# A new planner's order, with its engine and buffer choices, for a fused attention and squared-ReLU kernel

## The chip, the cores and the metric

The kernel runs on one core of a Trainium2 chip. The metric is the device time of one execution in microseconds (us), lower is better. Before the change, three runs took 608.24, 609.28 and 611.04 us, median 609.28. The engines are named as in the profile: PE is TensorE's matmuls, PEld its weight loads, DVE is VectorE, ACT is ScalarE, POOL is GpSimd, and SP is the engine whose queue issues every transfer (DMA) of this kernel.

## What is computed

Attention with rotary embedding on q, k, v of shape (4 batches, 8 heads, 576 rows, 64), and then a two-layer network on its 2304 x 512 output. In short:

```python
q_rot, k_rot = (rotate(q), rotate(k))
scores = scale * np.matmul(q_rot, k_rot.transpose(0, 1, 3, 2))
attn = softmax(scores)                 # with the row maximum taken off
x = heads_side_by_side(np.matmul(attn, v))     # (2304, 512)
h = x @ w_in                           # (512, 2048)
g = s * np.maximum(h, 0.0) ** 2 + b
return g @ w_out                       # (2048, 512)
```

## The kernel before

The 32 heads are worked on as 16 pairs (pair = two heads of one batch). A pair's 576 rows are 8 tiles of 128 rows (four of each head) and a ninth, number 8, that holds the last 64 rows of both heads. The output rows are nine units: units 0 to 7 are halves of a batch's first 512 rows, and unit 8 is the last 64 rows of all four batches. The network's hidden layer has 16 blocks of 128 columns.

The work is cut into **pieces**, of one to some tens of instructions each. The ones that the text names are these.

- Loads: `load_x` (L530) brings q, k or v of a pair, `load_w` (L447) one of 32 weight chunks of 512 KB, `load_tab` (L533, L534) the rotation table and an identity.
- Weights: `w_low`, `w_rebias` and `w_join` rebuild float32 words from the 8-byte numbers of a chunk, `w_gram` (L477) is a product that bounds their size, and later `w_hi` and `w_lo` split each chunk into two float16 parts.
- Pairs: `rotate` is three steps (L589, L591, L593). Pairs 0 to 3 then go in float32: `qk_T` transposes q or k on TensorE (L766, L769) and `qk_ev` copies the result out. The other pairs are split into float16 by `qk_hi` and `qk_lo`, transposed by a DMA, and k's swapped copy is made by another (`swap_k`). `v_hi` and `v_lo` split v.
- Scores: `s_pair` (L654) or `s_tile` (L672, L673) makes them, `s_max` (L679, L681) the row maximum, `s_exp` the exponentials and row sums, `p_s` and `p_r` (L708) the reciprocal. `p_a` and `p_b` split a tile of probabilities into two float16 parts, and `p_t` and `p_tt` (L738, L742) are transposes by DMA of the result. Some tiles of pairs 0 to 3 are transposed on TensorE instead: `p_diag` makes a diagonal matrix, `p_T` (L794, L796) multiplies with it and `p_ev` copies out. `pv_sum` (L759) and `pv32` (L813) are the products with v, `o_out` writes them into the unit's x.
- Network: `x_norm`, `x_add` (two steps, L845), `x_sum` (L851), `x_scale`, `x_hi` and `x_lo` scale and split a unit's x. `mlp_in` (L886) is one hidden block, `mlp_r` applies ReLU and square, `g_hi` and `g_lo` (L904) split the result, `mlp_out` (L962) adds a block to an output row part, `out_sum` scales it and `store` (L982) writes it out. Unit 0 does this in float32 (`mlp_in0` L912, `mlp_out0` L929). Unit 7 is the last; its output has a full-width part 0 (128 x 512) and two half-width parts 1 and 2 (128 x 256), other units have two full-width ones.

Casts, activations and scaled copies go through helpers, so many pieces share the lines L411, L413 and L416 (`ts_`, `stt`) and L419 (`act`); they are told apart by their tiles.

What sets the order: a function `plan` lists all 2,644 pieces with what they depend on and the engines on which they may run. A search that ran ahead of time wrote three strings into the file. `ORDER` has two characters for each piece, and the program issues the pieces in just that order; each engine then runs its own in that order, waiting at each for what it needs. `PICKS` names an engine (S for ScalarE, V for VectorE, G for GpSimd) for each piece with a choice, and `SLOTS` a buffer for each tile whose kind has several. The main lines (L1005 to L1016) are:

```python
        for n in order:
            x = work[n]
...
                if k[0] in BUFS and k not in at:
                    at[k] = int(next(where))
...
            if x["pick"]:
                a = (*a, pick[x["fn"], a])
```

The choices that matter here are in `plan`:

```python
        add((DVE, POOL), "x_add", u, steps=2, w=[("g", ("n", u))])
            add((DVE, POOL), "g_lo", u, f, r=[("hr", c)], w=[("g", c)])
                add((ACT, DVE, POOL), "p_a", *c, r=[("p", c), ("r", (pr, g))], p=[("pab", c)])
```

Of the kernel before, what the change touches and what calls it, by code (L numbers as in the profile page):

```python
# [42 lines left out]
    "JwJjD-KND1JpB_JxJEJ4BtJqCSJrBsJsJkD3BJEIKAEaBOJtBuCOEMKBJ5JlB2JuEWJyBPKOKCCNBUJzEkBZJ6J0CPJ7CUBaCBKPKaJmJ1ElKQCTJ8BqKbJ9"
    "BvJ2EyCVEJKcKDKiK8J3KXD7KECCacKdCDKeBwCHKFB4afKfKjK9aeB3CEK-adbuD4BxEBKrB5agKkKgCXahCIKYKsaoK_KlKzKZKhKmCJLAJ-ECamK0KnBz"
    "LiKtEDKoEECKapByEFEGLjENEYCAKuCFLkB0anLBKvEOEPLIKwK1aqCGEwK2arKpLVCYCZKxbvaiKqKGK3LJajLWbwLCJ_awLlK4LKazEmCiEZCdCaLFEzbx"
    "byEbLmbzEhLnb0KHLGayEiKyLHLoakLLKIEQK5alLMLTLNaxCtCeLUFLEjCbERCWa0LuLOa1b1LQK6CjLXL7asK7LPCcLYLvLcLZEcbIEdLRL8bFLDEeCvLd"
# [1046 lines left out]
```

## Time and profile before

| | us |
|---|---|
| median of three runs | 609.28 |
| the profiled execution's own time | 608.72 |
| its span, first to last instruction | 606.9 |
| PE busy | 579.2 (95%) |
| DVE busy | 468.6 (77%) |
| ACT busy | 396.2 (65%) |
| POOL busy | 152.0 (25%) |

The profile is of one execution. A row of a group of instructions gives its line, engine, operation, tiles written and read, shapes and count, then its busy time, and what its engine waited for just before. A matmul's end is modelled and overlaps the next one's start, so a stretch in which PE is busy throughout can still hold short waits.

### The profile page before, as it was taken

The numbers are of one execution on the slowest core, as the hardware profiler recorded it, in microseconds if no ns is written. First come the engines' busy times: TensorE is split into PE (matmuls) and PEld (weight loads), VectorE is DVE, ScalarE is ACT, GpSimd is POOL, SyncE is SP. The second block draws the span as 40 slices with busy tenths as digits, with TensorE's granted clock in tenths as the row PEclk, the third lists the DMA queues.
The fourth block names the chain that finished last, engine by engine and source line by source line (L and its number), as shares of the span: only waits on it lengthen the run. The fifth ranks groups of instructions, "written<-read, shape, count | busy, mean of one in ns | idle before, by whom it ended". The sixth has DMA issues, their size and how long they took to land.

```text
span 606.9 us, 12363 instructions
## 1 busy us (share of the span) xinstructions
PE 579.2 (95%) x4655; PEld 394.4 (65%) x4655; DVE 468.6 (77%) x972; ACT 396.2 (65%) x832; POOL 152.0 (25%) x147
## 2 busy tenths in 40 slices
PE   2778999999999999999999999999999999999997
PEld 1556776675776658665866676567666686666774
DVE  5988999998999999888998879988858743413212
ACT  3687897878789887888766767666653555432430
POOL 0155432432213333232413322122010101210100
PEclk9989999999999999999999999999999999999999
DMA  8887899996976477898969498687641223540010
GB/s 339 288 293 252 230 227 196 230 188 145 167 136 170 103 151 176 162 229 184 184 113 172 115 194 153 122 169 155 138 111 22 59 65 50 114 79 1 1 36 35
DMA packets 210011, 90.32 MB, mean 149 GB/s; under 512 B 192288, under 2 KB 196768, under 8 KB 209952
## 3 DMA queue, kind: packets, MB, share of 16 engines
q1 hardware_dynamic: 209952, 89.54, 64.4%
q8 instruction: 36, 0.59, 0.4%
q14 instruction: 23, 0.19, 0.1%
HBM read 31.97 MB, written 4.72 MB: 60 GB/s over the span
## 4 chain that ended last, share of the span: by engine, by line
PE 76%; DVE 11%; DMA 4%; ACT 3%; issue 2%; POOL 2%; SPq 0%; DVEq 0%; ACTq 0%; POOLq 0%
PE px L886 24%; PE po L962 21%; PE px L759 8%; PE s L672 6%; PE po L929 4%; PE px L912 3%; PE s L654 3%; DMA pt<-pab 3%; DVE wio L416 2%; DVE pab L416 2%; PE s L962 2%; DVE s L681 1%; POOL g L845 1%; PE po L794 1%; PE px L477 1%
## 5 line engine op out<-in xcount | busy, mean ns | idle before, releaser
L886 PE MATMUL px<-xa,wio 128*128 128x256 f16 x1536 | 181.4, 273 | 0.0
L962 PE MATMUL po<-wio,g 128*128 128x512 f16 x720 | 172.0, 380 | 0.0
L886 PEld LDWEIGHTS <-wio 128*128 128x128 f16 x1536 | 147.3, 98 | 31.0 <-issue 2.4
L419 ACT ACTIVATE p<-s,nm 128x576 f32<-128x576 f32 x144 | 105.5, 734 | 60.1 <-DVE s L681 34.4
L416 DVE SCALAR_TENSOR_TENSOR pab<-p,sum,pab 128x576 f16<-128x576 f32 x136 | 113.3, 844 | 17.6 <-ACT pab L419 10.0
L962 PEld LDWEIGHTS <-g 128*128 128x128 f16 x816 | 75.9, 98 | 73.3 <-issue 3.8
L681 DVE TENSOR_SCALAR_CACHE_REDUCE s<-s,sc 128x576 f32<-128x576 f32 x108 | 87.8, 819 | 13.7 <-PE s L673 12.0
L413 POOL TENSOR_SCALAR pab<-p,sum 128x576 f16<-128x576 f32 x53 | 50.0, 948 | 157.2 <-DVE sum L708 84.1
L419 ACT ACTIVATE hr<-px,xc 128x512 f32<-128x512 f32 x64 | 43.7, 683 | 67.2 <-PE px L886 58.3
L904 POOL TENSOR_TENSOR g<-hr,g 128x512 f16<-128x512 f32 x29 | 36.8, 1272 | 165.8 <-ACT g L419 90.4
L419 ACT ACTIVATE pab<-p,sum 128x576 f16<-128x576 f32 x64 | 48.1, 765 | 7.9 <-DVE sum L708 6.2
L759 PE MATMUL px<-pt,v 128*64 128x320 f16 (+2 forms) x640 | 50.9, 281 | 1.8 <-DMA pt<-pab 1.6
L419 ACT ACTIVATE hr<-hr 128x512 f32<-128x512 f32 x68 | 42.7, 628 | 1.7
L759 PEld LDWEIGHTS <-v 128*64 128x64 f16 x640 | 34.5, 110 | 13.2 <-issue 10.2
L904 DVE TENSOR_TENSOR g<-hr,g 128x512 f16<-128x512 f32 x35 | 26.0, 742 | 21.9 <-ACT g L419 21.5
L672 PE MATMUL s<-qkT 128*128 128x512 f16 (+1 forms) x120 | 41.5, 383 | 0.0
L672 PE MATMUL s<-kS,qkT 128*128 128x512 f16 (+1 forms) x120 | 41.4, 381 | 0.0
L672 PEld LDWEIGHTS <-qkT 128*128 128x128 f16 (+1 forms) x240 | 22.4, 100 | 24.8 <-issue 4.9
L783 DVE CAST g<-hr 128x512 f16<-128x512 f32 x27 | 11.3, 423 | 35.0 <-ACT hr L419 20.5
L912 PE MATMUL px<-x,wio 128*128 128x128 f32 x256 | 33.0, 281 | 0.0
L912 PEld LDWEIGHTS px<-x,wio 128*128 128x128 f32 x256 | 30.4, 192 | 3.4 <-issue 2.1
L416 DVE SCALAR_TENSOR_TENSOR wio<-x,wio 128x512 uint32<-128x512 uint32 x32 | 26.2, 823 | 5.7 <-POOL wio L413 5.4
(153 smaller groups left out, 831.3 us busy)
## 6 DMA issues: line engine op xcount, KB each, us to landing
x<-in_moe_w_in_dram SPq DMA_DIRECT2D x16, 512.0 KB, 5.1
x<-in_moe_w_out_dram SPq DMA_DIRECT2D x16, 512.0 KB, 4.6
st_v<-in_v_dram SPq DMA_DIRECT2D x16, 320.0 KB, 3.8
st_q<-in_q_dram SPq DMA_DIRECT2D x16, 288.0 KB, 3.8
st_k<-in_k_dram SPq DMA_DIRECT2D x16, 288.0 KB, 4.1
out_dram<-o SPq DMA_DIRECT2D x7, 512.0 KB, 4.0
kS<-qkT SPq DMA_DIRECT2D x24, 144.0 KB, 2.8
pt<-pab SPq DMA_TRANSPOSE x152, 2.9
```

The lines of the kernel that those rows point to most:

```text
L413: eng.tensor_scalar(out=out, in0=in0, scalar1=s1, scalar2=s2, op0=op0, op1=op1)
L416: nc.vector.scalar_tensor_tensor(out=out, in0=in0, scalar=scalar, in1=in1, op0=op0, op1=op1)
L419: nc.scalar.activation(out=out, in_=in_, func=func, **kw)
L654: nc.tensor.matmul(ps[h][:, to], d["qF"][hh, t * P:(t + 1) * P], d["kF"][hh, keys], start=True, stop=True)
L672: nc.tensor.matmul(ps[rows, MAIN:2 * MAIN], lhs, kk[:, h:8:2], start=(n == 0), stop=(n == 1))
L681: nc.vector.tensor_scalar(out=T["s"], in0=T["s"], scalar1=st[pr]["es"], scalar2=None, op0=ALU.mult, op1=ALU.min, accum_out=T["nm"])
L759: nc.tensor.matmul(o[64 * h:64 * h + 64, c], v_rows(pr, h, k, z), p_rows(pr, 2 * (i // 4) + h)[:, k, c], start=((z, k) == todo[0]), stop=( ...
L886: nc.tensor.matmul(ph, w16[0][:, f, wz, cc], X["xa"][:, xz, c], start=(c == 0 and n == 0), stop=(c == NC - 1 and n == 2))
L904: (nc.vector if eng == DVE else nc.gpsimd).tensor_tensor(out=g[:, 1], in0=r, in1=g[:, 0], op=ALU.subtract)
L912: nc.tensor.matmul(ph, wi[:, f + 1, c * P:(c + 1) * P], xs[0]["x"][:, c, j * P:(j + 1) * P], start=(c == 0), stop=(c == NC - 1))
L929: nc.tensor.matmul(X["po"][:, j * DM:(j + 1) * DM], gs["h", j, f - f % 4][:, f % 4 * P:(f % 4 + 1) * P], wo[:, f + 1], start=(n == 1), sto ...
L962: nc.tensor.matmul(po, g[:, gz, jj], w16[1][:, f, wz, to], start=(n == 1 and i == 0), stop=(n == NF and i == 2))
```

## The change

Only the three strings change. `plan`, all pieces and all buffers' counts and sizes stay. Cut to the first lines of each string:

```diff
--- before.py
+++ after.py
 ORDER = (
-    "AvA0AAC0CzADDPDQAOA2A1AxA3AwAZAyAzApC6C7C8C3AEC_C4C5DADCDTAFC9AGDWA4AeC-DDDUAPDBI0DXAQDVAaAqI1ARI2I8BbAbDZDYI3ArAcI9DIDd"
-    "AgDEAIDbI-DJC1DfDKDRDFBdDGDaI4A5AfDNI5DHDcAsAJDLAhBgDODmATAKDeAHBcI6DMDnBeJFI_DoAkJAI7ALDSJGBFDgBiBhC2D8JNJHDhAUJIJOJJBj"
...
+    "C0AACzApDCAvDPADA0C6C7C3C8ArC4C_AqAsC5DQAxAODIC9AwDTDAAyC-DUBbAFI0DBDJAEDfDVA1I1AGI2DWAZI3DZI8AQAPA2DXDaDdARBdDYBgI4A3Db"
+    "I5BcDFAII9DKDeDGDNAbBeAaDHAHBFDcC1DmDODLDDAcBhDRDnBiAeDgDMBjAJJFAkDpI-AKDoI6JNBHBGALJOC2JGATI7DsD8DqJHI_DrDEJIJAAMDtBIDS"
...
 )
...
 PICKS = (
-    "SSSGSSVGSGSGSSSVVGSVSSGGGSSGVVSSVVSSVVSSVVSSVVVSSGGGGGGSGVVGGSVGGSSVVSSGVVSGGVVSGGVVSGGVVSSGVVSGVVVSSSVVVSSVVSGSSGSVSSSS"
...
+    "SSGVSGSSSGGVGGSVSSVVSGGGSGGSGGSSVVSSVVSSVVSSVVSVGGSGVGSGSVVSSSVGSSSGVSSSVVSGSVVVSVVVGSSVVSSVVVGGSVGSSSVVVGSVGGVSSSSSSSSS"
...
 )
...
 SLOTS = (
-    "010021131000100001120001030101111123110010202100013101023000100210133000111110021011201100203130011001202111030013103030"
...
+    "000111230100001101010001201100013101011020232110010230003131102000011010120331010001110002100131200102130101110132012001"
...
 )
...
```

Decoded with the unchanged `plan`, both orders hold the same 2,644 pieces, and in both no piece stands before one that it depends on. Of the 530 choices of an engine 239 go to ScalarE (233 before), 168 to VectorE (166) and 123 to GpSimd (131); of 1,040 buffer choices 591 differ. On TensorE the order of 645 of 705 pieces differs, on average by 5 places and at most by 46. What the text comes back to:

| | before | after |
|---|---|---|
| first transfers | weight chunks 8 and 9, table and identity, q of pair 0, k of pair 0, weight chunk 0 | q of pair 0, table and identity, k of pair 0, weight chunk 7, q of pair 1, weight chunk 8 |
| first on TensorE | `w_gram` 8, `qk_T` q and k of pair 0 | `qk_T` q and k of pair 0, `s_pair` of pair 0 |
| first on VectorE | two `w_join`, then the rotation of q and k of pair 0 | the rotation: two steps of q, one of k, the last of q, one of k, a `w_join`, the last of k |
| `x_add` on GpSimd | units 1, 2, 4, 5, 7, 8 | unit 1 |
| `rotate` on GpSimd | q and k of pair 4, q of pair 6 | q of pairs 4, 6, 13 and 15, k of pair 7 |
| `p_diag` on GpSimd | 5 of 8 | 3 of 8 |
| `p_a` on ScalarE, VectorE, GpSimd | 64, 19, 53 | 67, 25, 44 |
| `w_hi` on the same | 21, 3, 8 | 14, 7, 11 |
| last product and store of unit 7 | part 2 (128 x 256) | part 0 (128 x 512) |

## Rows read from the trace of the kernel before

**Rows 1.** The page's parts 1 and 2: busy us, and TensorE's busy tenths in 40 slices.

```profile
PE 579.2 (95%) x4655; PEld 394.4 (65%) x4655; DVE 468.6 (77%) x972; ACT 396.2 (65%) x832; POOL 152.0 (25%) x147
PE   2778999999999999999999999999999999999997
```

**Rows 2.** Busy time by stretch: stretch, length, busy us of each engine (instructions), granted clock, DMA.

```profile
0.00:60.00 60.00, 40.07 (x306) 28.73 (x307) 48.81 (x90) 39.77 (x85) 18.05 (x21) 0.97 0.84 293
60.00:165.00 105.00, 103.08 (x853) 71.93 (x851) 99.28 (x207) 82.42 (x185) 37.16 (x37) 1.00 0.92 200
165.00:290.00 125.00, 124.05 (x1008) 81.28 (x1006) 117.80 (x252) 104.82 (x221) 37.43 (x33) 1.00 0.73 164
290.00:450.00 160.00, 159.10 (x1328) 106.72 (x1327) 140.12 (x297) 107.67 (x235) 40.07 (x39) 1.00 0.74 147
450.00:607.00 157.00, 152.94 (x1171) 105.78 (x1169) 62.55 (x130) 61.54 (x109) 19.24 (x18) 1.00 0.24 49
```

**Rows 3.** The chain that ended last, in order of time: start us, us, what.

```profile
67.54 1.39 PE px L813 x20
...
163.39 5.24 PE px L886 x48
...
288.32 2.62 PE px L886 x24
...
482.14 2.59 PE po L962 x12
```

**Rows 4.** Timeline of VectorE where units 1 and 3 begin: start us, us, instruction.

```profile
161.49 1.28 DVE L416 SCALAR_TENSOR_TENSOR xa<-x,xs,xa 128x1024 f16<-128x1024 f32 x1
...
164.49 1.54 DVE L416 SCALAR_TENSOR_TENSOR pab<-p,sum,pab 128x576 f16<-128x576 f32 x2
...
286.38 1.28 DVE L416 SCALAR_TENSOR_TENSOR xa<-x,xs,xa 128x1024 f16<-128x1024 f32 x1
```

**Rows 5.** Timeline of the start, SP's queue, VectorE and TensorE.

```profile
0.74 0.87 SPq L447 DMA_DIRECT2D x<-in_moe_w_in_dram  x2
...
2.60 0.74 SPq L530 DMA_DIRECT2D st_q<-in_q_dram  x1
...
6.59 0.69 DVE L416 SCALAR_TENSOR_TENSOR wio<-x,wio 128x512 uint32<-128x512 uint32 x1 [5.41 <-POOL wio L413]
...
8.22 0.75 DVE L589 TENSOR_TENSOR z<-st_q,tab 128x576 f32<-128x576 f32 x1
...
10.61 1.12 PE L766 MATMUL s<-ident,st_q 128*128 128x128 f32 x4 [1.64 <-DVE st_q L593]
```

**Rows 6.** Busy time of the stretch from 5 to 10 us (columns as in rows 2).

```profile
5.00:10.00 5.00, 0.61 (x4) 0.34 (x4) 3.01 (x5) 1.99 (x4) 0.64 (x1) 1.00 1.03 400
```

**Rows 7.** The instructions of line 845: duration ns min/median/max, first and last start, forms.

```profile
L845 POOL TENSOR_TENSOR g<-g x12: 668/1152/1571, 155.8 to 545.4; 128x512 bf16<-128x512 bf16 x6, 128x256 bf16<-128x256 bf16 x6
L845 DVE TENSOR_TENSOR g<-g x4: 291/359/426, 280.6 to 460.0; 128x512 bf16<-128x512 bf16 x2, 128x256 bf16<-128x256 bf16 x2
```

**Rows 8.** TensorE's waits after 60 us: us in total, times, longest us.

```profile
PE px L759 <- DMA pt<-pab: 1.6, 4, 0.7
PE px L851 <- POOL g L845: 1.5, 3, 0.8
```

**Rows 9.** Timeline of the end: the full-width and the last half-width out_sum.

```profile
600.85 0.75 DVE L416 SCALAR_TENSOR_TENSOR o<-po,xc,bcs 128x512 f32<-128x512 f32 x1 [4.70 <-PE po L962]
...
603.53 0.48 DVE L416 SCALAR_TENSOR_TENSOR hr<-s,xc,bcs 128x256 f32<-128x256 f32 x1 [1.22 <-PE s L962]
```

**Rows 10.** DMA issues: tiles, queue, operation, count, KB each, median us to landing.

```profile
out_dram<-hr SPq DMA_DIRECT2D x2, 128.0 KB, 1.9
out_dram<-o SPq DMA_DIRECT2D x1, 256.0 KB, 2.6
```

**Rows 11.** Timeline of VectorE: a rotation step that runs beside one of GpSimd's.

```profile
36.74 1.97 DVE L593 TENSOR_TENSOR st_q<-st_q,z 128x576 f32<-128x576 f32 x1
```

More of the change, by code (lines that the diff above doesn't have):

```diff
@@ L43 @@
[L43 to L46, printed above, removed]
@@ new lines @@
+    "D1KMJVJ4JqBoJrEID-JsJxJkBZJyBpBUEaCNBJBaJtCSKACOKNKBCPKOJlJ5JuB2D6EJJzBtBOBsJ0KCJ6BuEkCBKaJ1EWKDKPKXJmKEJ7J2KbCUB3BPKiKc"
+    "CTBvBqKFKjK8KQKdJ3D7KkCCCDafbuJ8EBKeK9adCEK-acElBxB4KfJ9aeK_CVEZKrKlKgCHKmagBwB5ahKYELKsapKhKzByaoKnKtEManBzKoKZB0KuamK0"
+    "CtD4CFK1CiaqLiLAJ-arCAK2LjECaiK3CGLkKvK4KpLBEDEhLIJ_KqEECJEFLlEGLCCIEPajKGLJENbvakCjLVKwalLmLKCKLnLWCXawbwKxFMEbazbxLoCu"
+    "LFbyEOCvCkbzCwEwb0KHLGaxLTKyEmLUasb1K5LHayEiLuEQa0CoCYEjFLatLLERLXEzLML7LQaua1LYLvLNLcavLRKIE7K6LwLdLZMILDE8K7EcClbFMJLS"
@@ new lines @@
+    "bGb2EdLaMKbIEeLeEfLOL8bHEgb3MLFOLPLrb4CZMMb5bJLEa9MNLsbKb6L5a8LbEpb7a7EnCaa6L6Eyb8MOCdCqbLL9EqLta2E9a-ExMRESFYa_CpFZLfL-"
+    "LxMCL_LyMSL2MACeLzCWMfMBCbMTa3CrL3a4LpL0Mga5CcLqCfMDMULhLgCgE0L4EoB6CQE-B1MhCLbAL1CRMib9bBE_MjB7MEMkCxMVMoCsbQMlMWFKbPMm"
+    "ErMXFaM3b-CyMYMcMZMFFAM4ETNFM5MdE1MuMnb_MHMGMpbRNGcAMQMvEtE2bME3MwE4MaMPbNFNE5MxE6MycBbSMzMbcCChM0bTM6MqbUcDFDCmM7cEbaFP"
+    "MeFEbZM8CncFM9EsbbM-NHNCM_NlEucGFVbONmNIbccHACFBEUNiNJbdNKNDMrNLbeNjNncINANOFQbCM1NPNkbDcJMsM2NoNMNUcKNXNpFRNVNqNNbVFWNY"
@@ new lines @@
+    "NWbWNBcLMtFHN1FXbkN2NtNQcMbjNuNZblcNNENaN3EVNybmcOABNbFCNfbXFSFFFTNrNcOAFUbncPNRbocUNzcQFlNgN0cRcVbYN4NvNScWN5NddBODcXbf"
+    "FGcYFbcZdCOBbgOENhOCdDbhFccSN6dEbiNeFddFdGOFbpdHdIdJNsdKOGbqdLFedMbrcTFIOHdNbscaOLF_OTFfcbbtOQOIN7dOccN9OUbEdPFmcdNTFkFo"
+    "N-NwOVceORdQdRcfPMN_NxOMd2dScgFhdTONPNdZGCchOSN8OJdYciOWPOOXEvFgOedad3PPcjdbF-GMOKdcOhckFndUFyd4djGNFid5cld6diOicmOYOfd7"
+    "ObdtGOOjdddkcndVdldXdfPQOcPROuFzOOOgFjcoPSdhOPOdcpOkdWcqeBGadmcrGAdnOvOxcsdsOlOyOmOpctdeOwFvdgOZdudoOqdvO_OaOzeAFwcuOnOr"
@@ new lines @@
+    "O8GBcvdpO0FxOocwdrFJdweUeCdxPAFpeVO1O9PBO5cxO-dqO6eDPYcyeWOsPCPDczPEPHPZO2dzGJPaPVPIeEd1OtPFeFPjeXFqd9PWPGeLPkPXc0PJF0Pl"
+    "eKO3Frc1O4Pmd_Fsc2FtPbFuPcPndyF3PdO7QAGKPod0PeG0Pgd8eYPhd-GDF4P0PpeMPKPqP1GZPrPuc3eZeNeHQBeOPTP2eGePGEeIc4PfGFGGPsQCeJPv"
+    "QLF1PieRc5PLQOehQMPwc6QPQNeiPtQQejP9F2QRP3eQc7P4PUQSGHP-QTQWekQoGdGIeTP5elF5emc8enP6ebeoP_epQXeSc9eqeaerQDesQEQpQzQFPxQq"
+    "etQIF6Q0QcF7QUeuF8QdQ1GLevPzGRGYc-PyQVQJede5c_QeQGdAewRQQKGPexecQfGQQlfMeyQYQmezRRe4QnP7QgeeQhfNefe6QHQre7QsQiREGbGSP8fD"
@@ new lines @@
+    "Gce8RSRFe9GTfCQtGjfOe0QwfPQxe1GyGzQuQ2RGGee3GffEGgGme_fFRHRNRIQ3QZfQQ4GnRJGhGiGoQ5fXG1QvGkGrQ6ROQ7e2QkRKe-Q8ReRPQyfWfGQ-"
+    "GlfHRTQaQ9RfRbG3fARUQ_QbRVfYfIRcRAfZfhGpRgGVRdQjfBGqRYfJRWHMfgG9RhGsfKRifRGtRjR9G-fiR6fLfjR7RBRmGUR-R8RkRvRnRDRMGvfTRZfa"
+    "fVRoG_G2fbfrRwRCRLHAfqRxR_HBRaRsfkSAF9G4fdflRXSYSBRtSFfSSCSZfURlRuG5SDfcSbSGSaHOffGwScfsfnRyftRzSKG6HNG7HPG8feHCSdRpfuSL"
+    "fvHFHGR3f1RqSEHDR4gBf0GWR0RrR1fmGuf2gCSNgDHEf3gEfpHnf4gFSHfogGSMSef5SfSOfwSgfygHgISPgJR2f6gKHJSQfxgLSjgMfzSkR5f7SRgNSVSr"
@@ new lines @@
+    "HmHQf9HHSWgOSsHaStgZHbShSoS5SpgPHXSqgYSugQGXHIgRS6S2SSSIHceggagSgbSTgTHRgjS3SiSJHYS7HSgiSXS4HZHTS8SvHUTXSwHVSUS9gcf8S-f_"
+    "HpTUHWS_SzHdSlg3gkTYgdglTVg2HKTZSxHfTBTGg4hKTHg5GxTWhLHgTag6f-Smg7S0TkSnSyTbTfgUhMTlTIgWTATChNgVTgTmTJS1gXTcTnHegfgmTKgs"
+    "TDToTLTpT-gnHoTMgtHqIBTNTdICTRH0T_geUATtH1TEguTugvTSTOUMTTghUNggHxThgogwHygqUOHLgpHrTPTwgrTqTvTQhBTxTFTegxTyhAUPUQIEURgA"
+    "TzUST7IAgzT8Hhg1T0T9T1T4UYg9IFUZH2U0UBhCUCTiU1hDUDUGT5gyT2U2T6g0UEUag8IcTjHsUmHtUHhhUjg_UIUkU3hEhVUnUlhFUFHzUog-UVUphOT3"
@@ L84 @@
+    "nonrnunx"
 )
 PICKS = (
[L87 to L90 removed]
@@ L92 @@
+    "VVSVSGSGVGVGVGVSVGSVSVSVSVSGVVSGVVVGSVVGVGSVSVVVSV"
 )
 SLOTS = (
[L95 to L98 removed]
@@ L104 @@
+    "00025120100011100110011001100200101002000110312100101010102000110100121000110100"
 )
```

79 lines of the change are left out of this document (28 added, 51 removed).

## The prediction, made before the changed kernel ran

> **What bounds the kernel now.** I read the busy shares first, then the stretches, then the chain, then the waits. TensorE is busy 95% of the 606.9 us span, and its slices are full from the fifth on [rows 1]. By stretches it idles 19.9 us of the first 60, 1.9 of the next 105, 1.0 and 0.9 in the two after these, and 4.1 in the last, which holds the final stores [rows 2]. So nearly all that an order can win without taking work away is in the first 60 us, at the end, and in short waits. VectorE has little to spare either: it idles 5.7 us of 60 to 165, 7.2 of 165 to 290, and only then falls off [rows 2]. Until about 290 us two engines are nearly full, and a piece moved on VectorE shifts what TensorE can start.
>
> TensorE's products run at their full pace once fed: 48 first-layer products take 5.24 us, or 109 ns each, and 12 second-layer ones 2.59 us, or 216 ns [rows 3]. No product is removed or added, so that time is fixed. The profiled execution took 608.72 us with a span of 606.9, and the median of the three runs, 609.28, lies 0.56 above it. I sum against 608.72 and add 0.56 at the end. About 0.5%, or 3 us, is what a measurement of this kernel can tell from no change.
>
> **How the orders are compared.** Both orders decode to the same 2,644 pieces: 705 on TensorE and 286 on the DMA queue in each; VectorE goes from 859 to 862, ScalarE from 651 to 657, GpSimd from 143 to 134. Sums of work hardly move, so only the order counts. For a chosen product I count what stands ahead of it: on TensorE all pieces before it, on VectorE all pieces up to the last one that it needs. A piece costs the distance from its start to the next start where nothing waits. Two p_b together last 1.54 us [rows 4], so one costs about 0.73.
>
> **The start.** Before, the queue sends two weight chunks (1,024 KB), the table, the identity and then q of pair 0; VectorE's first work is two w_join, from 6.59, the first rotation step of q starts at 8.22 and TensorE transposes q at 10.61 [rows 5]. After, q and the table go first and the first weight chunk fourth. The stretch from 5 to 10 us moves 400 GB/s [rows 6], so 1,024 KB less ahead is worth up to 2.6 us: the first rotation step can start near 5.6, which is VectorE's first work and 1.0 sooner than 6.59. The transpose of q came 2.39 us after that step's start and now has one more step ahead (k's first, 0.75 us): 8.75, or 1.9 sooner. Between 1.0 and 1.9 I take 1.5 for VectorE; the ends are 0 and 2.6.
>
> **The order up to unit 3,** at three places.
> (a) The last float32 value product, pv32(3,0), which starts at 67.54 [rows 3]. VectorE has 84 pieces ahead instead of 90: two s_max, two p_ev, two w_join, one p_s and one p_r fewer, two rotation steps more. That is 3.0 us less; TensorE has two w_gram (0.4 us) less. With the early start TensorE would have lost 4.1 us less by here.
> (b) The first product of unit 1, at 163.39 [rows 3], behind x_lo, which starts at 161.49 and takes 1.28 [rows 4]. VectorE has 286 pieces ahead instead of 277, net 3.0 us: two w_lo, two qk_lo, three p_a, two w_hi, three p_s, one p_r more, two p_ev, one w_low and one x_hi fewer. With the 1.5 of the start, x_lo ends 1.5 later, but four mlp_out0 (3.4 us) more stand behind TensorE: it has lost 1.9 us less.
> (c) The first product of unit 3, at 288.32 [rows 3], behind x_lo at 286.38 [rows 4]. VectorE has 0.9 us more ahead, so with the start it is 0.6 sooner, but TensorE has an s_tile, an mlp_out and an all_sum (1.2 us) less behind it: it has lost 0.6 more.
> I take 2.3 us less, near (b) and a little towards (a), since in (c) much of VectorE's 7.2 idle us of that stretch is waiting for others, and its time there is no firm bound. The ends are 4.1 less and 0.6 more.
>
> **x_add.** It moves from GpSimd to VectorE in units 2, 4, 5, 7 and 8; unit 1 stays. The two steps take some 1.15 us each at the median on GpSimd and 0.36 on VectorE [rows 7]. After 60 us TensorE waits 1.5 us for it in three places, the longest 0.8 [rows 8]. One of the three is unit 1's. I take 1.2 less; the ends are 1.5 and 0. The cost is about 0.7 us of VectorE per unit; two of the five are in (c)'s count, and the other three fall where VectorE idles 20 us of 160 and more [rows 2].
>
> **Transfers.** TensorE waits 1.6 us in four places for a transposed probability tile [rows 8]. This is what a planner with truer transfer times can remove, and in four products between 95 and 155 us (pairs 0 to 3, second half) 2.2 to 3.5 us more TensorE work stands ahead of the product than before. But every transfer goes through the one SP queue, and moved loads can make such waits anew. The trace has no price for that; the nearest is the longest of these waits, 0.8, and three new ones would cost 2.4. I take half of the old ones away, 0.8 less; the ends are 1.6 less and 2.4 more.
>
> **Engine picks.** 15 g_hi go to VectorE and 17 to ScalarE, 42 p_a leave GpSimd and 33 come to it, among others. They lie beside products and I cost them at nothing: the first-layer product of a pair of blocks stands 3.6 us of TensorE work or more ahead of the second-layer product that needs its result, at the least 2.9 before. Where that cover is gone the wait is of the size of x_add's, and lies in the 2.4 above.
>
> **The end.** Before, the last product is the half-width part 2: its out_sum takes 0.48 us [rows 9] and its 128 KB store 1.9 [rows 10]. After, the full-width part 0 is last: 0.75 [rows 9] and 2.6 for 256 KB [rows 10]. Nothing covers it: 1.0 us more. In the Trainium skill, "DMA: Bandwidth & Descriptors", section "Anatomy of one DMA — SWDGE (gpsimd) path", a transfer costs some 2.0 us plus its bytes at 436 GB/s; by that estimate the stores differ by 0.3 us, not 0.7, and this term would be 0.6. It has its measured durations here, and they stand.
>
> **Sum:** -2.3 - 1.2 - 0.8 + 1.0 = -3.3 us. 608.7 - 3.3 = 605.4, and with 0.56, 606.0.
>
> **Rivals.**
> 1. The gain stops at unit 3. If VectorE reaches (c) no sooner than counted there, the early gain is given back: +0.6 - 1.2 + 1.0 = +0.4, no change in transfers, 609.7. For it: VectorE is 94% busy from 165 to 290 [rows 2]. Against: its idle time there.
> 2. Slower: GpSimd's pieces slow VectorE more than before. A rotation step that takes 0.75 us alone took 1.97 beside a GpSimd piece [rows 5, 11]. The order gives GpSimd's pieces other neighbours, and moves pair 7's rotation of k to it before (c). If this costs VectorE 4 us more before (c), or some four such meetings, TensorE starts unit 3 that much later: 0.6 + 4.0 - 1.2 + 1.0 = +4.4, 613.7. It decides from about 3 us on. Against: GpSimd has nine pieces fewer. The Trainium skill, "SBUF — State Buffer", section "Who interferes with whom", has VectorE and GpSimd share one port pair as an exclusive lock, so that whoever comes second is blocked for the whole piece. The row agrees with it.
> 3. All of it lands: -4.1 - 1.5 - 1.6 + 1.0 = -6.2, 603.1. For it: (a), and the larger cover ahead of the value products. Against: (c).
>
> **How the numbers follow.** The forecast, a gain of 1 to 5 us, has 0.60; rival 1 has 0.17, rival 2 0.11, rival 3 0.12. A little over half of the forecast lies beyond 3 us: faster 0.47, same 0.42, slower 0.11. The range goes from below rival 3, since new covers may hide more than I count, to between rivals 1 and 2: 601.5 to 611.5.
>
> **What would show it.** The transpose of q starts near 8.8 and not 10.6; pv32(3,0) starts before 66; unit 1's first product starts near 165 with TensorE's idle time of the first 165 us some 2 us below the 21.8 of before; TensorE waits for x_add in unit 1 alone; some 3.4 us and not 2.4 lie between the start of the last out_sum and the landing of its store. I am wrong if VectorE reaches x_lo of unit 3 after 288 us (rivals 1 and 2), if a wait of over 2 us stands on TensorE after 60 us, or if the first 60 us hold 19 us of idle TensorE or more.

## The result, and the profile after

Four runs of the changed kernel took 601.03 to 603.72 us, median 603.48; four of the kernel before beside them had the median 610.16. The ratio is 0.988, with a 95% interval of 0.985 to 0.992: 1.2% faster, or 6.7 us. The profiled execution went from 608.72 to 603.72, its span from 606.9 to 601.9. A second set of six runs, told below, gave 602.54 and 0.989.

The page's parts 1 and 2 after, beside [rows 1]:

```profile
span 601.9 us, 12378 instructions
PE 575.6 (96%) x4655; PEld 391.7 (65%) x4655; DVE 467.4 (78%) x975; ACT 400.6 (67%) x838; POOL 143.8 (24%) x138
PE   2799999899999999999999999999999999999997
```

The stretches after, with the columns of [rows 2]; the last is shorter by the 5 us won:

```profile
0.00:60.00 60.00, 43.37 (x363) 30.76 (x363) 50.13 (x97) 42.85 (x94) 16.09 (x21) 1.00 0.90 308
60.00:165.00 105.00, 102.03 (x818) 70.41 (x818) 101.80 (x211) 84.99 (x185) 36.71 (x33) 1.00 0.88 195
165.00:290.00 125.00, 124.43 (x1052) 82.69 (x1048) 120.40 (x256) 101.69 (x216) 32.45 (x31) 1.00 0.79 164
290.00:450.00 160.00, 158.56 (x1304) 105.67 (x1304) 139.60 (x296) 111.91 (x243) 40.56 (x37) 1.00 0.71 146
450.00:602.00 152.00, 147.17 (x1132) 102.17 (x1129) 55.44 (x119) 59.11 (x103) 18.01 (x17) 1.00 0.21 49
```

TensorE's idle time is 16.6, 3.0, 0.6, 1.4 and 4.8 us, 1.4 less in all than [rows 2] give. The other 3.6 of the 5.0 are busy time (579.2 to 575.6): products that ran slower, and waits too short to break a busy stretch. Idle time alone therefore misses most of the gain, and from here on I use **lost time**. For each TensorE piece it is the distance from its start to the next start, less the distance that only a tenth of its kind undercut in the kernel before. The sum, with the first start, is the time that TensorE has lost so far against a run in which it is always fed. Before it is 31.0 us by 60 us, 39.2 by 160, 42.9 by 300 and 48.9 at the end; after 26.4, 34.3, 39.0 and 43.1. The gain is 4.6 by 60, 4.9 by 160, 3.9 by 300 and 5.8 at the last product; from there to the span's end the new kernel takes 0.8 more.

The three places of the prediction, in the timelines of TensorE and VectorE after:

```profile
9.36 1.11 PE L766 MATMUL s<-ident,st_q 128*128 128x128 f32 x4 [9.36 <-DVE st_q L593]
...
61.18 1.46 PE L813 MATMUL px<-pt,st_v 128*64 128x128 f32 x20
...
159.77 1.26 DVE L416 SCALAR_TENSOR_TENSOR xa<-x,xs,xa 128x1024 f16<-128x1024 f32 x1
161.71 2.78 PE L886 MATMUL px<-xa,wio 128*128 128x256 f16 x24
...
280.05 1.26 DVE L416 SCALAR_TENSOR_TENSOR xa<-x,xs,xa 128x1024 f16<-128x1024 f32 x1
```

The last float32 value product starts 6.3 us sooner (before, 67.47 in this timeline; the 67.54 of [rows 3] is the chain's); VectorE reaches x_lo of units 1 and 3 1.7 and 6.3 us sooner than at 161.49 and 286.38 [rows 4].

TensorE's waits after 60 us (us in total, times, longest), beside [rows 8]:

```profile
PE s L672 <- ACT p L419: 1.8, 2, 1.4
PE po L929 <- DVE wio L416: 1.6, 1, 1.6
PE s L661 <- ACT p L419: 0.7, 1, 0.7
PE px L759 <- DVE wmx L480: 0.6, 2, 0.3
```

The waits for transposed tiles and for x_add are gone. The three for x_add in [rows 8] were those of units 2, 4 and 7 (0.27, 0.82 and 0.38 us), all of them moved to VectorE. Unit 1's product never waited for it; its wait before was 0.3 us for ScalarE:

```profile
PE px L851 <- ACT wio L419: 0.3, 1, 0.3
```

New are 1.6 us at 116 us, where mlp_out0 waits for w_join(1,12), and 1.4 at 298, where s_tile(11,0) waits for a buffer that s_exp frees.

One thing of the start is only seen in finer stretches. Before, busy time and granted clock around 40 us, and TensorE's timeline:

```profile
36.00:38.00 2.00, 0.42 (x8) 0.25 (x5) 2.00 (x3) 2.00 (x7) 1.31 (x1) 1.00 0.89 255
38.00:40.00 2.00, 1.18 (x12) 0.84 (x12) 2.00 (x4) 0.81 (x3) 0.10 (x1) 1.00 0.85 267
40.00:42.00 2.00, 1.71 (x5) 1.22 (x6) 1.84 (x5) 2.00 (x5) 1.57 (x2) 0.60 0.80 252
42.00:44.00 2.00, 2.00 (x19) 1.79 (x15) 1.35 (x3) 1.19 (x3) 1.92 (x3) 0.54 1.01 377
```

```profile
38.82 0.63 PE L766 MATMUL s<-ident,st_q 128*128 128x128 f32 x4 [2.39 <-ACT wio L419]
...
40.33 2.52 PE L654 MATMUL s<-qkT 64*128 64x512 f32 x8 [0.29 <-DVE sum L708]
```

The rotation step of 1.97 us beside a GpSimd piece [rows 11] ends at 38.71. TensorE, which needs it next, is idle 2.39 us until 38.82 (the row names another piece as the one waited for). Then the granted clock of the two stretches is 0.60 and 0.54, so most of them ran at the lower of its two levels (1.2 of 2.4 GHz), and s_pair(2,0) takes 2.52 us. After, TensorE is busy without a break from 36 to 44 us, the clock is 1.00 and the same s_pair takes 1.30:

```profile
37.10 1.30 PE L654 MATMUL s<-qkT 64*128 64x512 f32 x8
```

Most of the lead at 60 us is made here. At 36 us lost time is 23.1 before and 23.3 after; at 45 us it is 28.0 and 24.0. The runs told below give the spread: five traces with the old start have 23.1 to 24.4 at 36 us (mean 23.9) and 26.3 to 28.0 at 45 (27.3), seven with the new start 21.5 to 23.3 (22.6) and 23.1 to 24.1 (23.6). So about 1 us of lead stands at 36 us, and some 2.4 more are made from there to 45. The new order has q of pair 3 rotated by 33.5 us, where it was 38.71, and k of pair 4 on VectorE, so that this meeting with GpSimd cannot happen.

The fall of the clock is not what separates the medians, though. Of 86 runs of the kernel before, made beside the experiments, 19 have a mean granted clock of 0.999 or 1.00, so no such fall, and their median is 609.9 us. In 44 it is 0.996 to 0.998, which is what one fall like this gives (the two stretches lack 1.7 us of full clock, of 607), and their median is 609.6; in the 23 with less, 611.7. A kernel before without the fall is still 6 us behind the changed one.

In the first 60 us VectorE's pieces are 4.1 us longer in sum than the tenth-shortest of their kind before, and 1.7 after. Over the whole execution the sums are some 30 us in both, a little more after: the meetings with GpSimd have moved away from the start, not gone.

### The profile page after: what moved, and what is told of

Its sections match the earlier page's. It is cut to its first block, busy times and chain, and to the rows that moved or that the text cites. A ratio compares the mean times of both kernels' runs of the same rounds, so it can differ in the third digit from the quotient of the medians.

```text
span 601.9 us, 12378 instructions
## 1 busy us (share of the span) xinstructions
PE 575.6 (96%) x4655; PEld 391.7 (65%) x4655; DVE 467.4 (78%) x975; ACT 400.6 (67%) x838; POOL 143.8 (24%) x138
## 4 chain that ended last, share of the span: by engine, by line
PE 83%; DVE 7%; DMA 4%; ACT 3%; issue 2%; POOL 1%; SPq 0%; DVEq 0%; ACTq 0%
PE px L886 28%; PE po L962 25%; PE px L759 8%; PE s L672 8%; PE po L929 4%; PE px L912 4%; DMA x<-in_moe_w_in_dram 2%; DMA x<-in_moe_w_out_dram 2%; PE s L962 2%; DVE wio L416 2%; PE s L654 2%; ACT p L419 1%; PE s L673 1%; DVE pab L416 1%; ACT x L419 1%
## 5 line engine op out<-in xcount | busy, mean ns | idle before, releaser
L416 DVE SCALAR_TENSOR_TENSOR pab<-p,sum,pab 128x576 f16<-128x576 f32 x136 | 118.7, 887 | 8.1 <-ACT pab L419 4.7
L904 POOL TENSOR_TENSOR g<-hr,g 128x512 f16<-128x512 f32 x36 | 44.5, 1239 | 175.2 <-DVE g L783 85.4
L413 POOL TENSOR_SCALAR pab<-p,sum 128x576 f16<-128x576 f32 x44 | 38.9, 887 | 165.6 <-DVE sum L708 114.9
L419 ACT ACTIVATE pab<-p,sum 128x576 f16<-128x576 f32 x67 | 50.5, 767 | 18.2 <-DVE sum L708 16.4
L759 PE MATMUL px<-pt,v 128*64 128x320 f16 (+2 forms) x640 | 49.0, 281 | 0.6 <-DVE wmx L480 0.6
L904 DVE TENSOR_TENSOR g<-hr,g 128x512 f16<-128x512 f32 x28 | 19.2, 688 | 36.1 <-ACT g L419 35.8
L419 ACT ACTIVATE hr<-hr 128x512 f32<-128x512 f32 x68 | 42.7, 629 | 1.7
L759 PEld LDWEIGHTS <-v 128*64 128x64 f16 x640 | 32.8, 110 | 11.2 <-issue 8.4
L672 PEld LDWEIGHTS <-qkT 128*128 128x128 f16 (+1 forms) x240 | 22.6, 100 | 23.8 <-issue 4.8
L419 ACT ACTIVATE g<-hr 128x512 f16<-128x512 f32 x39 | 24.2, 625 | 13.6 <-PE po L962 10.9
L783 DVE CAST g<-hr 128x512 f16<-128x512 f32 x25 | 10.5, 419 | 23.9 <-PE po L962 15.0
```

What stands on the lines that cost most here:

```text
L413: eng.tensor_scalar(out=out, in0=in0, scalar1=s1, scalar2=s2, op0=op0, op1=op1)
L416: nc.vector.scalar_tensor_tensor(out=out, in0=in0, scalar=scalar, in1=in1, op0=op0, op1=op1)
L419: nc.scalar.activation(out=out, in_=in_, func=func, **kw)
L672: nc.tensor.matmul(ps[rows, MAIN:2 * MAIN], lhs, kk[:, h:8:2], start=(n == 0), stop=(n == 1))
L759: nc.tensor.matmul(o[64 * h:64 * h + 64, c], v_rows(pr, h, k, z), p_rows(pr, 2 * (i // 4) + h)[:, k, c], start=((z, k) == todo[0]), stop=( ...
L904: (nc.vector if eng == DVE else nc.gpsimd).tensor_tensor(out=g[:, 1], in0=r, in1=g[:, 0], op=ALU.subtract)
```

## The experiments

**The question.** The gain is twice the forecast, and most of it stands by 60 us. My theory after this reading ("start"): the new start wins 4 to 5 us and the rest keeps them. Its rivals: the engines chosen make the gain; or it is spread over the order, and a start's lead is given back by an order that wasn't made for it.

ORDER is unreadable as text, so the edits are given as pieces in the order of issue. The table has every run: ratio to the kernel before in the same set of runs, with its interval, and the lost time of one profiled execution at 60, 100, 160 and 300 us and at the last product.

| run | median us | ratio (95%) | 60 | 100 | 160 | 300 | end |
|---|---|---|---|---|---|---|---|
| before | 610 | | 31.0 | 34.0 | 39.2 | 42.9 | 48.9 |
| after | 603.48 | 0.988 (0.985 to 0.992) | 26.4 | 28.6 | 34.3 | 39.0 | 43.1 |
| new_again | 602.54 | 0.989 (0.985 to 0.992) | 25.2 | 27.3 | 31.2 | 36.3 | 40.4 |
| new_start_old_rest | 612.40 | 1.004 (1.002 to 1.006) | 26.5 | 34.5 | 39.2 | 44.0 | 52.5 |
| old_start_new_rest | 609.32 | 0.999 (0.997 to 1.001) | 29.3 | 34.8 | 38.3 | 42.9 | 47.2 |
| new_48_then_old | 609.80 | 1.001 (0.999 to 1.003) | 31.0 | 33.1 | 39.3 | 43.3 | 49.2 |
| old_52_then_new | 609.03 | 0.999 (0.997 to 1.001) | 28.5 | 31.0 | 37.0 | 41.4 | 45.6 |
| new_19_then_old | 611.44 | 1.003 (1.000 to 1.005) | 34.0 | 36.5 | 41.6 | 46.2 | 54.7 |
| new_picks_old_order | 628.29 | 1.030 (1.027 to 1.033) | 32.5 | 36.4 | 44.7 | 56.1 | 70.2 |
| x_add_back | 605.02 | 0.992 (0.990 to 0.995) | 25.5 | 27.7 | 33.1 | 38.0 | 43.9 |
| old_rotation_later | 609.12 | 0.999 (0.997 to 1.001) | 28.7 | 32.2 | 37.1 | 41.5 | 49.8 |
| new_48_chunk_later | 609.14 | 0.999 (0.996 to 1.001) | 28.9 | 31.3 | 37.4 | 42.0 | 50.6 |
| new_tuned | 601.19 | 0.987 (0.984 to 0.991) | 26.1 | 27.9 | 33.5 | 37.5 | 41.4 |
| old_products_later | 621.77 | 1.019 (1.016 to 1.021) | 29.0 | 32.8 | 40.5 | 46.8 | 62.0 |

### Halves: new start with old rest, and the reverse

```diff
 new_start_old_rest
+pieces 1 to 336 of the new order, with its engines
+the other 2,308, in the old order, with the old engines
```

> The first 336 pieces (some 70 us) in the new order, with its engines; the other 2,308 in the old order, with the old engines (31 buffer numbers differ at the seam). Theory 'start': the change wins its time in the first 70 us, where the trace after has TensorE 4.6 us less behind, and the rest keeps it: 4 to 5.5 us less than the kernel before. Rival 'spread': the early gain is given back where the old order waits for VectorE before unit 3 (rival 1 of the prediction), and the net gain comes from the later waits: 0 to 2 us less.

It came out 0.4% slower than the kernel before, so both expectations missed. The lead is there by 60 us (26.5) and gone by 100 (34.5). The waits of TensorE between 66 and 100 us:

```profile
PE px L912 <- DVE wmx L480: 3.4, 2, 1.8
PE s L661 <- ACT p L419: 2.0, 2, 1.6
```

Two products of unit 0 wait for the buffer that a w_max on VectorE frees, and s_tile(1,8) for s_exp. As I read it, the old order brings TensorE to these products when, after its own start, VectorE and ScalarE would be ready.

```diff
 old_start_new_rest
+pieces 1 to 336 of the old order, with its engines
+the other 2,308, in the new order, with the new engines
```

> The counterpart: the first 336 pieces old, the rest new. Theory 'start': only the later waits are won and the end lost (x_add and transposed tiles some 1.5 less, the end 0.7 more): 0 to 1.5 us less than the kernel before. Rival 'spread': 3 us less or more.

0.999: as "start" expected for this half, and together with the first half it contradicts it. The two halves should add up to 6.7 us; they add up to a loss. At this cut 31 buffer numbers of the old rest had to differ in the one, and 41 of the new rest in the other, so I cut again where the orders nearly agree.

```diff
 new_48_then_old (old_52_then_new: the other way round)
+pieces 1 to 219 of the new order, with its engines
+the other 2,425, in the old order, with the old engines and buffers
```

> A cleaner seam: the first 219 pieces (to about 48 us) in the new order with its engines, the rest old. Only three pieces stand on other sides of the cut in the two orders, and the old rest keeps all its buffers (the start's are renumbered to fit). Theory 'start': by the cut TensorE is some 3.8 us ahead of the kernel before and the rest keeps it: 3 to 4.5 us less. Rival 'given back': as with the cut at 336 pieces, the old rest waits at other places and is level again by 100 us: between 1 us less and 2.5 us more.

> The counterpart, cut at the same 219 pieces: old to about 52 us, then new. Theory 'start': the later part alone is worth 1 to 2 us: 0.5 to 2.5 us less than the kernel before. Rival 'given back': the new rest is what makes a start's lead last, and alone it wins 3 us less or more.

1.001 and 0.999. The first is level, as "given back" expected; the second, 0.6 us less, is the lower end of "start" and not the 3 us of "given back". Again the two don't add up. (The profiled execution of the second was its fastest, so its low row in the table stands for no median.) In the first, the trace shows how the lead goes within 7 us of the cut. Timelines of ScalarE and TensorE of new_48_then_old:

```profile
48.40 0.78 ACT L419 ACTIVATE pab<-p,sum 128x576 f16<-128x576 f32 x1 [0.83 <-DVE sum L708]
52.24 0.66 ACT L419 ACTIVATE wio<-x 128x512 uint32<-128x512 uint16 x1 [3.07 <-DMA x<-in_moe_w_out_dram]
...
53.99 0.69 ACT L419 ACTIVATE pt<-po 128x640 f32<-128x640 f32 x1
...
54.82 2.04 PE L794 MATMUL po<-dg,p 128*128 128x128 f32 x8 [3.49 <-ACT pt L419]
```

ScalarE waits 3.07 us for a weight chunk. Behind it in its queue stands p_ev, which TensorE needs: 3.49 us of wait at p_T(2,2). That product then takes 2.04 us for 1.1; the granted clock of 40 to 60 us is 0.83, so part of this stretch ran at the lower level. In the changed kernel w_low(1,2) is on VectorE and p_ev(2,0) goes ahead of that chunk; VectorE waits 1.0 us for the same chunk at 52.8, and TensorE 0.3 at p_T(2,2) and 0.5 at p_T(3,0).

### The first loads alone

```diff
 new_19_then_old
+pieces 1 to 51 of the new order, with its engines
+the other 2,593, in the old order, with the old engines and buffers
```

> The first 51 pieces new (to about 19 us: q, the table and k of pair 0 ahead of the weight chunks, the rotation ahead of the w_join), the rest old. By the prediction's term for the start VectorE gains 1.5 us that lasts: 1.5 us less. Rival: what is won at the first transposes (1.0 us at s_pair(0,0)) is lost again at the next ones, since two w_gram and two w_join that stood ahead only come later; by 30 us the two traces have TensorE at the same piece: within 0.7 us of the kernel before.

1.003, or 1.8 us more: both expectations missed. There is no gain, so the 1.5 us of the prediction's start don't last by themselves. It is no clean test of them, though: with the load of v of pair 1 moved by the cut, TensorE waited 5.6 us for it at 26.2 (v_gram).

### One meeting undone in the old order

```diff
 old_rotation_later
-  rotate(4, k) step 1
   load_x(4, q)
   ...
   p_diag(1, 2)
+  rotate(4, k) step 1
```

> The kernel before with one piece moved: the first rotation step of k of pair 4, on GpSimd, stands behind p_diag(1,2) in GpSimd's queue, so that it no longer starts at 36.7 us beside VectorE's last rotation step of q of pair 3, which took 1.97 us there. Theory 'meeting and clock': that step takes 0.75, TensorE's wait of 2.4 us at 38.8 shrinks by 1.2, and the granted clock does not fall to 0.6 and 0.54 between 40 and 44 us, which cost some 1.7: TensorE is 1.2 to 2.9 us ahead at 45 us; of the time 1 to 3 us less. Rival: the meeting only moves to VectorE's neighbours at 40 to 42 us, or the lead is lost by 100 us: within 0.7 us of the kernel before.

Timeline of VectorE, then the stretch from 40 to 44 us, of old_rotation_later:

```profile
37.27 0.76 DVE L593 TENSOR_TENSOR st_q<-st_q,z 128x576 f32<-128x576 f32 x1
```

```profile
40.00:42.00 2.00, 2.00 (x23) 1.76 (x21) 2.00 (x4) 1.64 (x4) 2.00 (x2) 1.00 1.00 309
42.00:44.00 2.00, 2.00 (x19) 1.37 (x18) 2.00 (x4) 1.91 (x5) 2.00 (x3) 1.00 0.95 283
```

The meeting is undone: the step takes 0.76 for 1.97, TensorE's wait is 1.22 for 2.39, the granted clock stays at 1.00, and TensorE is 2.3 us ahead by 60 us. But which of the two pieces comes first is a matter of hundredths of a us: before, GpSimd's starts at 36.69 and the step at 36.74. old_start_new_rest and old_52_then_new issue the same old order up to there, with GpSimd's piece where it was, and in both the step takes 0.75, since GpSimd's piece starts 0.29 and 0.01 after it. In the first it is the next VectorE piece that meets GpSimd, and the clock falls all the same. Its timeline of VectorE, and its stretch from 40 us:

```profile
36.71 0.75 DVE L593 TENSOR_TENSOR st_q<-st_q,z 128x576 f32<-128x576 f32 x1
37.38 1.91 DVE L416 SCALAR_TENSOR_TENSOR wio<-x,wio 128x512 uint32<-128x512 uint32 x1
...
40.00:42.00 2.00, 1.71 (x4) 0.90 (x6) 1.91 (x5) 0.90 (x2) 1.61 (x2) 0.54 0.87 264
```

The rival is right on the time: 0.999. The profiled execution keeps 2.1 us until 160, 1.4 at 300 and 0.2 at 400, and is behind by 450. Of that, 1.04 us are lost at the value product of pair 14. SP's queue and TensorE in the timeline:

```profile
434.51 0.58 SPq L982 DMA_DIRECT2D out_dram<-o  x1
435.13 4.46 SPq L738 DMA_TRANSPOSE pt<-pab  x2
439.64 1.28 SPq L742 DMA_TRANSPOSE pt<-pab  x1
...
442.61 0.96 PE L759 MATMUL px<-pt,v 128*64 128x320 f16 x10 [1.04 <-DMA pt<-pab]
```

Two transposes behind unit 4's store occupy the queue for 4.46 us, the last of the pair is issued at 439.64, and the product starts 0.13 us after it lands. In the kernel before the same two transposes take 3.49 us, and the product waits 0.06. Of all 32 products with v, 13 start before or within 0.3 us of the landing of their last transposed tile in the kernel before (12 here); after the change, 2, and 3 in the second profile. A TensorE that comes sooner can only wait longer at these, unless their transposes come sooner too.

### The chunk's wait at the seam mended

```diff
 new_48_chunk_later (against new_48_then_old)
-  w_low(1, 2); p_b(1, 3); pv32(1, 0); w_rebias(1, 2); s_max(3, 2); ...
+  p_b(1, 3); pv32(1, 0); s_max(3, 2); p_ev(2, 0); s_max(3, 0);
+  s_exp(3, 2); s_exp(3, 0); w_low(1, 2); w_rebias(1, 2); ...
```

> The kernel with the first 219 pieces new and the rest old, with one stretch of its seam mended: ScalarE's p_ev(2,0) and the s_exp of pair 3 go ahead of its two pieces on weight chunk (1,2), whose load landed at 52.22 us; before, ScalarE waited 3.07 us there with p_ev(2,0) queued behind, and TensorE 3.5 us at p_T(2,2) for it, the granted clock falling to 0.83. Theory 'landings': a start's lead lasts where no in-order queue holds a piece that TensorE needs behind one that waits for a load. TensorE is at least 3 us further at 60 us than with the seam unmended, and the kernel is 2.5 to 4.5 us faster than the kernel before. Rival 'given back anyway': the weight chunks land no sooner, so the lead is lost at the next chunk, and by 110 us TensorE is level with the kernel before: within 1 us of it.

p_T(2,2) no longer waits (49.95, for 54.82), but 0.999 is the rival's result, and TensorE is 2.1 us further at 60 us than with the seam unmended, not 3. The next wait, of 2.21 us, is at p_T(3,0), for GpSimd's diagonal, which waits for p_r(3,0) on VectorE, which stands behind w_join(1,2), which VectorE awaits for 2.13 us. The chunk's wait has changed its queue.

### The engines alone, and x_add

```diff
 new_picks_old_order
-PICKS of the old kernel
+PICKS of the new kernel (268 of 530 differ); ORDER and SLOTS old
```

> The old order and buffers with the new engine choices (268 of 530 differ). Theory 'order': the choices were made for another order, and their worth by themselves is nil or negative: between 1 us less and 4 us more than the kernel before. Rival 'engines': what was won is VectorE's pieces no longer beside GpSimd's (4.1 us of lengthened pieces in the first 60 us before, 1.7 after), so the choices bring at least 2 us by themselves.

3.0% slower, 18 us, far beyond what "order" allowed. The engines by themselves aren't the gain; in the old order they are a heavy loss. TensorE's waits after 60 us are mostly for s_exp, and after two of over 2 us the granted clock falls (0.57 from 331 to 335 us, 0.58 from 416 to 420):

```profile
PE s L672 <- ACT p L419: 10.7, 13, 2.3
PE px L759 <- DMA pt<-pab: 1.5, 4, 0.5
```

```diff
 x_add_back
-x_add of units 2, 4, 5, 7, 8: VectorE
+x_add of units 2, 4, 5, 7, 8: GpSimd
```

> The new kernel with x_add of units 2, 4, 5, 7 and 8 on GpSimd again. By the prediction's term TensorE waits for it again, some 0.5 to 0.9 us in two or three units: 1.2 us more than the new kernel (so some 4 to 5.5 less than the kernel before). Rival: the new order has enough TensorE work behind x_add to hide GpSimd's 1.2 us steps too: no difference to the new kernel, and no wait of TensorE for GpSimd at line 851 over 0.3 us.

605.0 and 0.992 lie 1.5 to 2.5 us above the two medians of the new kernel, with intervals that overlap. But TensorE does not wait for GpSimd at line 851 at all: the rival's second half holds. TensorE's waits after 60 us:

```profile
PE s L672 <- ACT p L419: 2.7, 4, 1.4
PE px L477 <- DVE wmx L480: 0.8, 1, 0.8
```

They are at s_tile for the most part, in four places where the new kernel has two or three. VectorE's pieces from 300 to 400 us are lengthened by 9.5 us in sum here, by 6.2 in the new kernel. So what x_add's move to VectorE buys, if anything, is fewer meetings, and not the waits that I priced; that the meetings cause the new s_tile waits is argued, not shown.

### The new kernel again, and three places altered

```diff
 new_again: no edit
 new_tuned
   w_rebias(1, 12)
+  w_join(1, 12)
   p_b(1, 7)
   ...
-  w_join(1, 12)
 and
+  s_max(11, 3)
   p_b(10, 2)
   ...
-  s_max(11, 3)
 and at the end of unit 7
-  ...; mlp_out of part 2; mlp_out of part 0; out_sum(0); store(0)
+  mlp_out of part 0; out_sum(0); store(0); eight mlp_out of parts 1 and 2, each with its out_sum and store
```

> The changed kernel itself once more, beside the others: ratio to the kernel before 0.988 again (603.5 against 610.2), and a second profile that shows which of its waits are the same each time. If the meetings of VectorE with GpSimd are a matter of chance, the waits of 1.6 us at 116 us (line 929) and 1.4 us at 298 us (line 672) stand at other places in it; if they come from the order, at the same ones.

> The changed kernel with three places of its order altered. First: w_join(1,12) goes ahead of p_b(1,7) on VectorE (TensorE's wait of 1.6 us at 116 us). Second: s_max(11,3) goes ahead of p_b(10,2), which took 1.81 us beside GpSimd there (the wait of 1.4 us at 298 us). Third: the full-width part 0 of unit 7 ends 8 half-width products before the end, and part 2 comes last, as in the kernel before. By my reading each place is read off by itself: the two waits go (1.6 and 1.4 us, some of it lost again at the next wait), and from the last product's end to the span's end 3.4 us instead of 4.2: 2 to 3.5 us less than the changed kernel. Rival: the meetings with GpSimd move to the pieces put in their place, and only the end's 0.8 is won.

new_again repeats the ratio. Of the two waits, that of s_tile(11,0) stands at the same piece in it, in the first profile, in x_add_back and in both runs with an old start and the new rest (idle 1.44 or 1.45 us each time): it comes from the order. That at 116 us doesn't return: the rotation step on GpSimd came after w_join(1,12) there, which took 0.69 us, and 0.6 us of wait stand at an s_pair at 112 instead. Timeline of VectorE and GpSimd at that place in the first profile:

```profile
113.92 1.41 POOL L591 TENSOR_TENSOR st_q<-st_q,tab 128x576 f32<-128x576 f32 x1 [0.46 <-ACT junk L419]
114.00 1.89 DVE L416 SCALAR_TENSOR_TENSOR wio<-x,wio 128x512 uint32<-128x512 uint32 x1
```

In new_tuned, the w_join goes first and takes 0.68; the rotation step meets qk_lo instead:

```profile
112.59 0.68 DVE L416 SCALAR_TENSOR_TENSOR wio<-x,wio 128x512 uint32<-128x512 uint32 x1
...
113.43 1.83 POOL L591 TENSOR_TENSOR st_q<-st_q,tab 128x576 f32<-128x576 f32 x1 [1.58 <-ACT junk L419]
113.92 1.96 DVE L416 SCALAR_TENSOR_TENSOR nat<-st_k,sc,nat 128x576 f16<-128x576 f32 x1
```

A VectorE piece of 0.68 us that starts 0.08 after GpSimd's of 1.41 takes 1.89, which is 0.1 short of the rest of GpSimd's piece and its own length together. The Trainium skill, "SBUF — State Buffer", section "Who interferes with whom", has the one that comes second blocked for the whole of the other's piece; this trace agrees to 0.1 us. The wait at mlp_out0 is gone, and 1.1 us of it come back at a w_gram at 116.8. At 298 us the idle time of 1.45 is 0.62. At the end, the last product's end is 3.5 us before the span's end, for 4.2:

```profile
593.42 0.75 DVE L416 SCALAR_TENSOR_TENSOR o<-po,xc,bcs 128x512 f32<-128x512 f32 x1 [5.28 <-PE po L962]
...
596.11 0.48 DVE L416 SCALAR_TENSOR_TENSOR hr<-s,xc,bcs 128x256 f32<-128x256 f32 x1 [0.24 <-PE s L962]
```

That is 0.7 at the end and 0.8 at 298 us, between the rival's count and mine; the median is 601.19 for 602.54, and the intervals overlap. It is the fastest kernel of the study, but not shown to be faster than the changed one.

### Wider covers in the old order

```diff
 old_products_later (against old_rotation_later), 18 times like
-  pv_sum(14, 3)
   mlp_in(5, 10)
+  pv_sum(14, 3)
```

> The old order with the moved rotation step of the run old_rotation_later, and 18 of the 32 products with v (those that started within 0.6 us of the landing of their last transposed tile in the traces with the old rest) moved back on TensorE by one to three pieces, 0.5 to 1.9 us of its work. Theory 'landings': a lead is given back where a product with v stands right behind its transposes (13 of 32 within 0.3 us before, 2 or 3 after); with the products moved the 2.3 us of lead at 60 us last, no wait of TensorE for a transposed tile over 0.4 us stands after 60 us, and the kernel is 2 to 3.5 us faster than the kernel before. Rival 'bound elsewhere': the old order's transposes follow TensorE's own pace, through s_exp and VectorE's p_b, so the waits come at other products or at s_tile instead, and the time stays within 1 us of the kernel before.

The waits for transposed tiles are gone, and the kernel is 1.9% slower. TensorE's waits from 60 to 600 us:

```profile
PE s L672 <- ACT p L419: 7.0, 9, 1.9
PE px L851 <- POOL g L845: 4.0, 4, 1.6
PE px L759 <- DMA pt<-pab: 0.5, 2, 0.2
```

The rival is right on the mechanism, but not on its size, for it allowed 1 us and the loss is 11.5: s_tile, which now comes sooner, waits 7.0 us for s_exp, and x_sum, whose x comes later, 4.0 for x_add. Moving these products alone does not help.

## Why the prediction was right or wrong

**The direction and the range hold**, 603.5 within 601.5 to 611.5; the gain is twice the forecast, and what happened is nearest to rival 3 (603.1).

**The start: right.** VectorE began at 4.77 us with q's first step, and not 5.6, but waited 1.56 us for k's load in between; the transpose of q came at 9.36 and, in the second profile, at 8.09, around the 8.75 forecast. Of the 1.5 us that this was to carry on, the first profile shows nothing at 36 us (lost time 23.3 for 23.1); over all traces with either start the lead there is 1.3 us.

**The order up to unit 3 is the step that failed.** At the products of (a), (b) and (c) TensorE was to have lost 4.1 us less, 1.9 less and 0.6 more; it had lost 5.8, 4.9 and 5.5 less (32.2 to 26.4, 39.2 to 34.3, 42.7 to 37.2). At (b) I took x_lo to end 1.5 us later, since VectorE had pieces worth 3.0 us more ahead of it; it came 1.7 sooner. My bound took VectorE's idle time as fixed. It was not: up to x_lo of unit 1 VectorE idled 16.9 us before and 13.1 after, and up to x_lo of unit 3 24.1 and 17.2. The pieces added went into time in which it had waited for others, as I had said it might, and then priced at almost nothing. So the term was -2.3 and measured -4.9 to -5.8. That (a) came out nearest is partly luck: in this pair of profiles 4.2 of its 5.8 us were made between 36 and 45 us, at one wait and at the clock's fall after it. The fall makes some 1.7 us of that (s_pair 1.2 longer, three w_gram 0.5 together). The prediction has no term for it, since the stretch of 60 us in [rows 2] shows 0.97; by the runs without a fall (609.9) it does not account for the 6.7 between the medians.

**x_add and transfers.** Both kinds of wait went, 1.5 and 1.6 us. For x_add I gave one of the three waits to unit 1, which had none, so 1.2 should have been 1.5; and I counted two of the moved units in (c), where only unit 2 is, which changes no number. The reason was wrong too: with x_add on GpSimd again there is no such wait either, so the order's cover removed it. For the transfers half was too little, and the one profile showed too little of them: old_rotation_later, with the old order's rest, waits 3.2 us for transposed tiles after 60 us. Four traces with the old rest and its products in place lose 6 us and more between 300 and 450, where the kernel before lost 3.9 in its profile; all four wait 0.9 to 1.1 us at pair 14's product, and none with the new rest does.

**Engine picks at nothing:** right in their own order alone. In the other they cost 18 us. The cover that I named (2.9 us and more in that order) did hide the pieces of g, for second-layer products wait 0.2 us in all; the waits came at s_tile, which I hadn't counted.

**The end: right in sign, 1.0 forecast, 0.8 measured.** From the last product's end to the span's end it took 4.25 us, for 3.48; from the start of the last out_sum to the landing of its store 3.24, for 2.41. The out_sum is 0.27 longer, as forecast, and the store 0.56 and not 0.7: it landed 2.46 us after its issue, for 1.90 of the 128 KB one. The 2.6 in [rows 10] came from a store that had two others beside it. The estimate by the Trainium skill's "DMA: Bandwidth & Descriptors", section "Anatomy of one DMA — SWDGE (gpsimd) path", was 0.3 for the stores; its figures are for transfers that GpSimd issues, and these are issued by SP.

**New waits** were priced at 0.8 each: the two longest measured 1.6 and 1.4. No wait of over 2 us came after 60, and the first 60 us held 16.6 idle us, as the forecast required. TensorE's idle time of the first 165 us fell by 2.2, for "some 2", but unit 1's first product started at 161.71 and not near 165: idle time alone misses what the clock and short waits give back.

**Rival 2** (GpSimd slows VectorE) is a true mechanism that went the other way at the start, and cost 1.6 us at 116.

What stays open: how the 6.7 us divide. No part that I carried over alone (start, rest, engines) won anything that can be measured, and two parts were never run alone: the new order with the old engines, and the 591 other buffer choices. The gain is shown only of the whole. Why a whole holds it is shown at single places, which do not add up to it: who stands behind a load in an in-order queue, and how close a product stands to its transposes.

## What to carry to other kernels

Where two engines are nearly full, as TensorE and VectorE are here until 290 us, don't expect a schedule's parts to add up. A lead of 4 us from one stretch was lost here as soon as the queues behind it had their pieces in another order, so judge an order whole. Before counting an engine's pieces as a bound, see what it idles for in that stretch; waiting time can take up added pieces at no cost. Read the start in stretches of 2 us with the granted clock, but check a fall seen in one profile against the mean clock of the other runs before putting it into the gain. For each consumer of a transfer, note the time from landing to start: products that stand within 0.3 us of it are places where a lead can be lost.

## What the runs showed that I had not expected

- With one VectorE step lengthened from 0.76 to 1.97 us TensorE idled 2.39 us, and the granted clock then was 0.60 and 0.54 between 40 and 44 us. With one GpSimd piece moved the wait was 1.22 and the clock 1.00, and yet the kernel was no faster; nor are the runs of the kernel before without a fall.
- Up to about 28 us products took nearly twice their later time in both kernels (before, s_pair 2.40 us at 15.1 and 1.36 at 30.0, p_T's first part 2.02 at 27.4 and 1.11 at 44.0) while the granted clock reads 1.00. The trace's records of the clock begin only at 30.2 us before and 29.7 after, and the column shows 1.00 where there is none. The durations change just there: after the change s_pair takes 2.24 us at 27.7, and p_T's first part 1.16 at 29.9.
- Two transposes behind a 512 KB store occupied SP's queue for 4.46 us in one trace and 3.49 in another, where one alone takes 1.3.
